# The last stage's begin set in another order: g products ahead of conversions, small weights in another PSUM bank, full products ahead of h products

## The chip, the core and the metric

The kernel runs on one core of one Trainium2 chip. Its engines are PE (matrix products), DVE, ACT and POOL (elementwise work) and SP, which issues the transfers. Each engine takes its instructions in the order of its own queue and waits at the first one whose inputs are not there. The metric is the time of one execution on the device in microseconds (us), the median of several runs.

## The reference

All of it is in float32; the weights of the last layer come as 64-bit floats and are converted on the chip.

```python
def reference(q, k, v, n_sink, window, phi, w1, w2, w_in, w_out):
    x = attention(q, k, v, n_sink, window)          # 4 x 768 tokens, 8 heads of 64
    x = x.reshape(3072, 512)
    logits = x @ phi                                # 3072 x 32
    d = softmax(logits, axis=0)
    s = (d.T @ x).reshape(8, 4, 512)
    o = relu(s @ w1) @ w2                           # 8 experts, 4 rows each
    x = softmax(logits, axis=1) @ o.reshape(32, 512)
    h = x @ w_in                                    # 3072 x 2048
    return (h - tanh(h)) @ w_out                    # 3072 x 512
```

## The kernel before

Attention, the routing and the experts take the first 227 us. The change concerns the last stage, the last two lines of the reference.

**The factors.** x has rank 32, so the kernel never forms it: the experts' output, transposed (`so`), is multiplied with w_in to a small matrix W of 32 x 2048, and h = c W with c the row softmax (`cT`). W is made by `w_mm(x)` in three parts, x = 0, 1, 2 with 128, 128 and 256 of 512 columns for each quarter of the partitions; they land in PSUM in `y`, in `cvt` and, the third, in the accumulator `o3` (`acc[3]`). `rows_a` (ACT) and `rows_b` (DVE) make from the first two the stationary tiles `wst0` and `wst1` of `hmm(0)` and `hmm(1)`; `whs_part` (ACT) and `wls_part` (DVE) split all three parts into a rounded and a rest part, from which `rows4` makes the other `wst`.

**A step.** Step s has a token chunk c of 512 tokens and a block f of 128 rows of w_out (f0 to f15). `hmm(s)` (PE, one matmul) makes h(s) in the PSUM bank `h0` or `h1`; `act_y(s)` makes on ACT a tanh and a square (`u`); `dve_part(s)` makes on DVE g(s), close to h - tanh(h) for the small h that occur; `split(s)` rounds it on ACT (`gh`) and takes the rest on POOL (`gl`). The product P(s) is `omm(s)`: for each of four accumulators `o0` to `o3` one matmul with gh and the block's `whi`, one with gh and `wlo`, one with gl and `whi`, 12 of 128x512. The first steps are (0,f0), (0,f1), (1,f0) to (1,f3), (0,f2) to (0,f5), (1,f4); at P1, P5 and P9 a group ends, the accumulators are evacuated (`evac`: o0 and o2 by ACT, o1 and o3 by DVE), and the next product overwrites them.

**A block.** Block f is converted from 64-bit words by `pre_conv(f, ops)`: four steps on DVE, "1", "2", "3", "g" (lines 116, 121, 126, 135), and a square on ACT, "s" (line 130). Then `wsplit(f)` takes POOL twice, for whi (line 1147) and wlo (line 1148). f0 and f1 are converted within SBUF, later ones by way of the PSUM bank `cvt`.

**The order.** Up to step 8 it is written out by hand: `step(s)` issues an older product `o`, then `hmm(s + 1)`, `act_y(s)`, `split(s - 1)`, then the evacuation of `o` if it ends a group, `dve_part(s)` with the conversions that `plan` has for s in between, and `wsplit`. `plan` is a table: step 3 has f2's second half, step 4 all of f3, steps 5 and 6 the halves of f4, step 7 all of f5, step 8 the first half of f6. From step 9 on a planner (`_Order`) sets the order of every engine by list scheduling: tasks carry a wished time, `LEAD`, `RCAST`, `TCAST`, `TLAG` and `TLAG2` say how far ahead of its use a thing is wished, and `BUSY` is the time for which it takes each engine to be still busy with the hand-written part. What it plans begins with P6. Behind step 31 the products go on with sums of blocks and of g's (a fast matrix product), to the end.

Of the kernel before, what the change touches and what calls it, by code (L numbers as in the profile page):

```python
# [10 lines left out]
F32 = mybir.dt.float32  # L11
# [5 lines left out]
AF = mybir.ActivationFunctionType  # L17
ALU = mybir.AluOpType
# [11 lines left out]
P = 128  # L30
# [26 lines left out]
CT = ((0, 4), (0, 6), (0, 7))  # L57
EPS_T = 0.0
US = {"tanh": 0.49, "mm": 0.2276, "h": 0.232, "act": 1.1, "cast": 0.49, "cast2": 0.3, "v": 0.6, "vs2": 0.34, "p": 1.26, "p2": 0.7, "pc": 0.7, "pch": 0.38, "ev": 0.49, "sq": 0.56}
LEAD, RCAST, SCAST, TCAST = 13.0, 6.0, 3.0, 6.0  # L60
RPS = 11
GGAP = 1.4
TLAG = 6.0
TLAG2 = 2.0
PAIRS = (((1, "P4"), (1, "P5")), ((1, "P7"), (1, "P1")), ((1, "P6"), (1, "P2")), ((1, "P3"), (2, "P4")),
         ((2, "P5"), (2, "P1")), ((2, "P7"), (2, "P6")), ((2, "P2"), (2, "P3")))
MULT = (("P4", "A22", "T4"), ("P5", "S1", "T1"), ("P7", "S3", "T3"), ("P1", "A11", "B11"), ("P6", "S2", "T2"), ("P2", "A12", "B21"), ("P3", "S4", "B22"))
# [77 lines left out]
class _Order:  # L145
# [1 line left out]
    LAT = {"PE": 0.2, "SP": 4.0, "ACT": 0.11, "DVE": 0.09, "POOL": 0.05}  # L147
    SELF = {"ACT": 0.12, "DVE": 0.12, "POOL": 0.12}
    PSUM = ("a0", "a1", "a2", "a3", "h0", "h1", "y", "cvt")
    BUSY = {"ACT": 0.3, "DVE": 2.7, "POOL": 3.8}  # L150

    def __init__(self):
        self.tasks = []
# [80 lines left out]
def tile_kernel(ctx: ExitStack, tc: tile.TileContext, qk, vv, v0, v0t, nw, phi, w1, w2,  # L234
                w_in, w_out, cst, gcst, out):
    nc = tc.nc
    PE, ACT, DVE, POOL, SP = nc.tensor, nc.scalar, nc.vector, nc.gpsimd, nc.sync
# [14 lines left out]
    def run(ctx, fast):  # L252
# [30 lines left out]
        for i in range(NR):  # L283
            pool, n = raw_p if i in RAW else ring2 if i in FREE else ring1, 1024 if i in HALF else 2048
# [739 lines left out]
        def raw_of(f):  # L1024
            return wraw[f % 6]
# [8 lines left out]
        acc = [pf.tile([P, 512], F32, name=f"o{t}") for t in range(4)]  # L1034
        y_t = pf.tile([P, 512], F32, name="y")
        cv_t = pf.tile([P, 512], F32, name="cvt")
# [3 lines left out]
        ca, cc = _cube(TAU * TAU)  # L1040
# [76 lines left out]
        whl = {}  # L1117
# [6 lines left out]
        wf, wf_b, cv_b, pcv = {}, [], [], {}  # L1124
# [8 lines left out]
        def pre_conv(f, ops):  # L1133
            if f not in pcv:
                wf[f] = wf_b[f if f < 8 else 8 + f % 3]
                pcv[f] = conv.start(raw_of(f), wf[f], cv_t if f > 1 else None)
            fns = {"1": conv.v1, "2": conv.v2, "3": conv.v3, "s": conv.sq, "g": conv.guard_dve,
                   "i": conv.ge_pool, "m": conv.mul_pool}
            for o in ops:
                fns[o](pcv[f])  # L1140

        def wsplit(f):
            hi, lo = whl[f]
            if f in WACT:
                ACT.copy(hi, wf[f])
            else:
                POOL.tensor_scalar(hi, wf[f], 1.0, 0.0, op0=ALU.mult, op1=ALU.add)  # L1147
            POOL.tensor_tensor(lo, wf[f], hi.bitcast(F32), op=ALU.subtract)
# [15 lines left out]
        for r in range(2):  # L1164
# [17 lines left out]
            for f in range(8):  # L1182
                for g in range(4):
                    i = 16 + 8 * r + 4 * (f // 4) + g
                    o, k = yo[NS * g:NS * g + NS, :], f
# [3 lines left out]
                    if k != f and f < 6:  # L1189
                        for x in range(2):  # L1190
                            PE.matmul(o[:, 256 * x:256 * x + 256], h, xt_t[2 * (k - 6) + x][:, 512:768],
                                      start=False, stop=False, skip_group_check=True)
# [17 lines left out]
            for x in range(2):  # L1210
# [3 lines left out]
                o = 16 * r  # L1214
# [7 lines left out]
        pre_conv(1, "s")  # L1222
        warm(WF[5])
        w_lo, w_n = (0, P, 2 * P), (P, P, 2 * P)
        W = [o[:, 0:n] for o, n in zip((y_t, cv_t, acc[3]), w_n)]
        w_st = [wa.tile([G3, n], F32R, name=f"wst{x}") for x, n in enumerate(w_n + (512, 512, 512))]

        def w_of(f):
            x, o = (f, 0) if f < 2 else (2, f - 2) if f < 4 else (2 + f // 4, f % 4)
            return w_st[x][:, P * o:P * o + P]  # L1230

        def w_mm(x):
            for f in range(4):
                for qd in range(4):
                    o = 512 * qd + w_lo[x]
                    PE.matmul(W[x][NS * qd:NS * qd + NS, :], so[f // 2][:, f % 2, :], win_t[:, f, o:o + w_n[x]],
                              start=f == 0, stop=f == 3)
# [14 lines left out]
        def h_of(s):  # L1252
            return h_b[s % 2]

        def hmm(s):
            c, f = steps[s][:2]
            PE.matmul(h_of(s), w_of(f), cT[0:G3, CK * c:CK * c + CK], start=True, stop=True)
# [1 line left out]
        w_mm(0)  # L1259
        rows_a(0)  # L1260
        rows_b(0)
        pre_conv(1, "12")
        w_mm(1)
        rows_a(1)
        hmm(0)
# [8 lines left out]
        def rows4(qd):  # L1274
            c = slice(0 if qd else 2 * P, 4 * P)
            for eng, g in ((POOL, 1), (DVE, 2), (ACT, 0)):
                dst = w_st[2 + qd][NS * g:NS * g + NS, :]
                src = (whs if g < 2 else wls)[NS * qd:NS * qd + NS, c]
                if eng is ACT:
                    ACT.copy(dst, src)  # L1280
                elif eng is DVE:
                    DVE.tensor_copy(dst, src)
                else:
                    POOL.tensor_scalar(dst, src.bitcast(F32), 1.0, 0.0, op0=ALU.mult, op1=ALU.add)

        def whs_part(x):
            ACT.copy(whs[:, w_lo[x]:w_lo[x] + w_n[x]], W[x])

        def wls_part(x):
            c = slice(w_lo[x], w_lo[x] + w_n[x])  # L1290
            DVE.tensor_tensor(wls[:, c], W[x], whs.bitcast(F32)[:, c], op=ALU.subtract)

# [8 lines left out]
        g_b, u_b = bufs("g", 3), bufs("u", 3)  # L1301
        gh_b, gl_b = bufs("gh", NG, F32R), bufs("gl", NG, F32R)
# [4 lines left out]
        def h_act(h, u, small):  # L1307
            if small:
                ACT.activation(h, h, AF.Tanh, scale=ca)
                ACT.activation(u, h, AF.Square, scale=cc ** 0.5)  # L1310
            else:
                ACT.activation(u, h, AF.Square)

        def act_y(s, small=True):
            h_act(h_of(s), u_b[s % 3], small)

        def split(s):
            g, gh, gl = g_b[s % 3], gh_b[s % NG], gl_b[s % NG]
            ACT.copy(gh, g)
            POOL.tensor_tensor(gl, g, gh.bitcast(F32), op=ALU.subtract)  # L1320

        def dve_part(s, small, fills):
            g_mul(h_of(s), u_b[s % 3], g_b[s % 3], small, fills)
# [26 lines left out]
        def omm(s, hi=True, lo=True, ts=range(4)):  # L1350
            c, f, first, last = steps[s]
            gh, gl = gh_b[s % NG], gl_b[s % NG]
            wh, wl = whl[f]

            def mm(t, a, w, start, stop):
                PE.matmul(acc[t], w[:, P * t:P * t + P], a, start=start, stop=stop)

            for t in ts:
                if hi:
                    mm(t, gh, wh, first, False)  # L1360
                    mm(t, gh, wl, False, False)
                if last and lo:
                    mm(t, gl, wh, False, True)
            if lo and not last:
                for t in ts:
                    mm(t, gl, wh, False, False)
# [40 lines left out]

        def step(s, small, pre):
            o = s - (DL + 1)
            if s < 5:  # L1410
                o = 1 if s == 3 else -1
            if o == 1:
                omm(1, lo=False, ts=(0, 1))
                for t in range(4):
                    omm(1, hi=False, ts=(t,))
                    if t < 2:
                        omm(1, lo=False, ts=(t + 2,))
            elif o >= 0:
                omm(o)
            hmm(s + 1)  # L1420
            todo = plan.get(s, ())
            fills = []
            act_y(s, small)
            split(s - 1)
            if o >= 0 and steps[o][3]:
                fills += evac(o)
            for f, ph in todo:
                fills += [lambda f=f, p=p: pre_conv(f, p) for p in ("3g" if ph else "12")]
                if not ph:
                    pre_conv(f, "s")  # L1430
            dve_part(s, small, fills)
            for f, ph in todo:
                if ph:
                    wsplit(f)
                    if f + 6 < 16:
                        wload(f + 6)
            if s in row_at:
                rows4(row_at[s])
# [3 lines left out]
        while turns:  # L1442
            n = 2 if s_ % 3 == 1 and turns[0][0] < 8 else 1
# [1 line left out]
            s_ += 1  # L1445

        act_y(0)
        w_mm(2)
        early.close()
        fq = ctx.enter_context(tc.tile_pool(name="fq", bufs=1))  # L1450
        w_split_tiles(fq, range(NB, 16))
        dve_part(0, True, ())
        pre_conv(1, "3")
        wload(7)
        split(0)
        pre_conv(1, "g")
        wsplit(1)
        hmm(1)
        omm(0, lo=False, ts=(0, 1, 2))
        whs_part(2)  # L1460
        wls_part(2)
        act_y(1)
        omm(0, lo=False, ts=(3,))
        dve_part(1, True, ())
        for x in range(2):
            whs_part(x)
            wls_part(x)
        hmm(2)
        omm(0, hi=False)
        split(1)  # L1470
        act_y(2)
        rows4(0)
        pre_conv(2, "1s")
        dve_part(2, True, (lambda: pre_conv(2, "2"),))
        hmm(3)
        for s in range(3, S0):
            step(s, True, True)
# [320 lines left out]
        for k, u in enumerate(units):  # L1798
            if u[0] != "r" and prods[u[1]][2] in ("T1", "T2"):
                j, o, i = nt % 3, 0 if u[1] == "P5" else 256, u[2]  # L1800
# [8 lines left out]
        for s, todo in plan.items():  # L1809
            if s < S0:  # L1810
                continue
            t = op(s - DL - 1)
            for e, (f, ph) in enumerate(todo):
# [12 lines left out]
                else:  # L1826
                    add(tb, "DVE", US["v"], rw + ["cvt"], ["cvt"], lambda cv=cv: conv.v3(cv))
                    add(tb + 0.5, "DVE", US["v"], [q, "cvt"], wn, lambda cv=cv: conv.guard_dve(cv))
                    hi, lo = whl[f]
# [4 lines left out]
                    if f >= 8:  # L1834
# [8 lines left out]

                        tb += TLAG if f < 13 else TLAG + TLAG2 * (f - 12)
                        tsub(tb, B1[:, lo_], [l_], B1[:, hi_], B1[:, lo_], [r_, l_])
# [6 lines left out]
        for s, qd in row_at.items():  # L1852
            if s >= S0:
                t = op(s - DL - 1)
# [7 lines left out]
        if fast:  # L1862
            t = op(18)
            add(t, "ACT", US["cast"], ["whs"], ["z"], lambda: ACT.activation(z, whs, AF.Square))
            add(t + 1, "DVE", US["v"], ["z"], ["wmax"], lambda: DVE.tensor_reduce(wmax, z, axis=AX.X, op=ALU.max))
            t = op(N + 100)
# [109 lines left out]
```

## Time and profile before

| | us |
|---|---|
| median of 3 runs | 507.75 |
| the runs | 507.40, 507.75, 510.46 |
| the profiled execution | 508.94 |
| span of its instructions | 507.0 |
| PE busy in the span | 480.7 (95%) |
| DVE, ACT, POOL busy | 414.6, 385.9, 301.6 |

The span is the time from the first to the last instruction of the profiled execution; the execution itself is 1.9 us longer. A matmul's busy time overlaps the next one's, so starts and not lengths tell how fast PE goes. A share of busy time is a mean over stages with different limits.

### The profile page before, as it was taken

To read this page: it belongs to the slowest core of one execution; us is meant where nothing else is said; L and a number is where in the kernel's file an instruction comes from. 1 tells how busy PE (TensorE), PEld (TensorE's weight loads), DVE (VectorE), ACT (ScalarE), POOL (GpSimd) and SP (SyncE) were. 2 spreads that over 40 slices of the span, in tenths; PEclk is the share of its full clock that TensorE was granted. 3 is DMA by queue.
4 is the path that set the end of the run, shared out by engine and by line. 5 is a ranking of instruction groups with operands and counts; after the bars stand their busy time and mean duration, and the time that the engine had idled before them with its cause. 6 is when DMAs were issued, how large, how long until landed. Compare 5 with 4: busy or idle time off the path is not lost.

```text
span 507.0 us, 10286 instructions
## 1 busy us (share of the span) xinstructions
PE 480.7 (95%) x3558; PEld 336.7 (66%) x3558; DVE 414.6 (82%) x826; ACT 385.9 (76%) x1084; POOL 301.6 (59%) x366
## 2 busy tenths in 40 slices
PE   8799999899998999798999999999999999999995
PEld 4565655555555633235688888888888888888884
DVE  2999998998998559659999999788858798965892
ACT  4889998998999414337898987998768998855750
POOL 0466755765654100005899998358747794789871
PEclk9999999999999999899999999999999999999998
DMA  8989976532385999994433000220000030100022
GB/s 298 414 332 349 348 300 244 178 132 95 106 296 185 307 313 404 410 406 154 124 100 109 1 0 2 83 84 1 1 0 0 2 125 1 41 2 0 1 85 87
DMA packets 22139, 77.60 MB, mean 153 GB/s; under 512 B 2882, under 2 KB 4034, under 8 KB 20162
## 3 DMA queue, kind: packets, MB, share of 16 engines
q1 hardware_dynamic: 22082, 76.89, 41.4%
q8 instruction: 29, 0.48, 0.4%
q14 instruction: 28, 0.23, 0.1%
HBM read 70.59 MB, written 6.29 MB: 152 GB/s over the span
## 4 chain that ended last, share of the span: by engine, by line
PE 66%; DVE 10%; ACT 10%; DMA 8%; POOL 3%; issue 2%; DVEq 0%; POOLq 0%; SPq 0%; ACTq 0%
PE o L1507 44%; DMA w<-in_w 4%; ACT w L702 4%; PE sc L672 3%; PE o L1088 3%; PE av L767 2%; DMA w<-in_qk 2%; PE h L1576 2%; ACT w L686 2%; DVE mx L693 2%; DMA w<-in_w_out 2%; PE pT L735 2%; DVE w L749 1%; PE mi L530 1%; POOL gl L1320 1%
## 5 line engine op out<-in xcount | busy, mean ns | idle before, releaser
L1507 PE MATMUL o<-gh,whi 128*128 128x512 f32 x232 | 91.2, 393 | 0.0
L1507 PE MATMUL o<-gh,wlo 128*128 128x512 f32 x232 | 90.9, 392 | 0.0
L712 POOL TENSOR_TENSOR w<-w,su 128x528 f32<-128x528 f32 x38 | 40.6, 1068 | 52.4 <-DVE su L709 37.5
L1507 PE MATMUL o<-gl,whi 128*128 128x512 f32 x232 | 71.6, 390 | 0.0
L1499 POOL TENSOR_TENSOR gl<-w,gh 128x512 fp32r<-128x512 f32 x39 | 51.3, 1322 | 26.5 <-ACT gh L1645 15.5
L702 ACT ACTIVATE w<-w,nb 128x132 f32<-128x132 f32 x152 | 59.6, 393 | 1.2
L1507 PEld LDWEIGHTS o<-gh,whi 128*128 128x128 f32 x232 | 43.7, 188 | 9.9 <-ACT mk L1705 0.2
L1507 PEld LDWEIGHTS o<-gh,wlo 128*128 128x128 f32 x232 | 43.6, 188 | 9.7
L1507 PEld LDWEIGHTS o<-gl,whi 128*128 128x128 f32 x232 | 43.6, 188 | 9.5
L767 PE MATMUL av<-w,w 128*64 128x256 f32 (+1 forms) x448 | 48.3, 344 | 0.0
L672 PE MATMUL sc<-w 64*64 64x200 f32 (+2 forms) x768 | 44.8, 331 | 2.3 <-DMA w<-in_qk 1.4
L1147 POOL TENSOR_SCALAR whi<-wx 128x512 fp32r<-128x512 f32 x6 | 3.7, 619 | 62.8 <-DMA w<-in_w_out 61.0
L767 PEld LDWEIGHTS av<-w,w 128*64 128x64 f32 x448 | 25.8, 136 | 16.4 <-issue 10.7
L672 PEld LDWEIGHTS sc<-w 64*64 64x64 f32 x768 | 26.1, 132 | 15.1 <-issue 9.9
L1334 DVE TENSOR_TENSOR h<-u,h 128x512 f32<-128x512 f32 x40 | 27.6, 691 | 10.0 <-ACT u L1588 9.9
L1645 ACT CAST gh<-h 128x512 fp32r<-128x512 f32 x40 | 23.6, 590 | 11.1 <-DVE w L1499 4.2
L749 DVE TENSOR_TENSOR w<-pT,c_t 128x512 f32<-128x512 f32 x46 | 31.3, 680 | 0.0
L1645 ACT CAST gh<-w 128x512 fp32r<-128x512 f32 x39 | 24.2, 621 | 7.9 <-PE o L1507 7.6
L686 ACT COPY w<-sc 128x264 f32<-128x264 f32 x63 | 21.1, 373 | 11.9 <-PE sc L803 6.1
L1499 DVE TENSOR_TENSOR gl<-h,gh 128x512 fp32r<-128x512 f32 x40 | 27.4, 685 | 2.7 <-ACT gh L1645 2.0
L702 ACT ACTIVATION_READ_ACCUMULATOR w<-w,nb 128x1 f32 x152 | 28.3, 186 | 0.0
L693 DVE TENSOR_REDUCE mx<-w 128x4 f32<-128x528 f32 x38 | 26.7, 703 | 1.3
(388 smaller groups left out, 1332.2 us busy)
## 6 DMA issues: line engine op xcount, KB each, us to landing
w<-in_w SPq DMA_DIRECT2D x30, 512.0 KB, 10.2
w<-in_w SPq DMA_DIRECT2D x14, 1024.0 KB, 6.5
w<-in_qk SPq DMA_DIRECT2D x16, 780.0 KB, 6.1
w<-in_w_out SPq DMA_DIRECT2D x16, 512.0 KB, 3.6
w<-in_vv SPq DMA_DIRECT2D x16, 384.0 KB, 4.0
w<-in_w_in SPq DMA_DIRECT2D x8, 512.0 KB, 4.8
out<-xt SPq DMA_DIRECT2D x12, 256.0 KB, 2.0
win_t<-in_w_in SPq DMA_DIRECT2D x4, 512.0 KB, 9.5
```

Source lines behind the costliest of these rows:

```text
L672: PE.matmul(sc_t[i][u][w, o:o + n], a[r, 64 * j:64 * j + 64], kslc(a, lo, n)[r, :], start=True, stop=True)
L686: ACT.copy(z, base)
L693: DVE.tensor_reduce(mx, Z, axis=AX.X, op=ALU.max)
L702: ACT.activation(Z[:, u, :], Z[:, u, :], AF.Exp, bias=nb[:, u:u + 1], scale=SCALE, accum_out=su[:, u, :])
L712: (POOL if i < NQ - 1 else DVE).tensor_tensor(Z, Z, su.to_broadcast([P, 4, CH]), op=ALU.mult)
L749: DVE.tensor_tensor(d[:, :, 0, :], src, mL, op=ALU.mult)
L767: PE.matmul(dst[r, :], v[:, t, r], l, start=start, stop=stop, skip_group_check=True)
L1088: PE.matmul(ha[x][NS * g:NS * g + NS, :], sT[f // 2][:, f % 2, :], ring_t(i + g, o, 512), start=f == 0, stop=f == 3)
L1334: DVE.tensor_tensor(g, u, h, op=ALU.mult)
L1499: td.any_of(at, {e: (us[e], lambda e=e: names[e].tensor_tensor(dst, a, b, op=alu), len(engs) > 1 or sbuf) for e in engs}, rd, wr)
L1507: PE.matmul(o, w, a, start=start, stop=stop)
L1645: add(at, "ACT", US["cast"], [gn], [f"gh{x}"], lambda: ACT.copy(gh_b[x], g))
```

## The change

`w_mm` takes a list of the parts f of its inner sum, and its third part now lands in the free columns of the bank `y` instead of in `o3`. h(1) is issued between the two halves of the third part, and its tanh and square are issued around the cast of g(0). g(0) and g(1) stand on DVE ahead of f1's conversion steps "2" and "3", "g". P0 is issued whole, its gh part and h(2) and its gl part. f1's whi is made by ACT, its wlo and gl(1) by DVE, and no longer by POOL. P1 takes all whi matmuls first. From step 4 on every hand-written product is issued one step sooner: `o = s - 2`, in steps 3 to 7, and step 8 issues none, so that P2 stands ahead of h(5), P3 ahead of h(6), to P5 ahead of h(8). `plan` is the same. f2's step "2" moves from the DVE part of step 2 to step 3, behind the evacuations. The planner's LEAD, TCAST, TLAG2 and BUSY have other values, by which it sets another order behind P6.

```diff
-LEAD, RCAST, SCAST, TCAST = 13.0, 6.0, 3.0, 6.0
+LEAD, RCAST, SCAST, TCAST = 10.0, 6.0, 3.0, 7.0
-TLAG2 = 2.0
+TLAG2 = 0.0
-    BUSY = {"ACT": 0.3, "DVE": 2.7, "POOL": 3.8}
+    BUSY = {"ACT": 0.8, "DVE": 3.7, "POOL": 4.2}
...
-        W = [o[:, 0:n] for o, n in zip((y_t, cv_t, acc[3]), w_n)]
+        W = [y_t[:, 0:P], cv_t[:, 0:P], y_t[:, P:3 * P]]
...
-        pre_conv(1, "12")
+        pre_conv(1, "1")
...
+        def h_tanh(s):
+            ACT.activation(h_of(s), h_of(s), AF.Tanh, scale=ca)
+
+        def h_sq(s):
+            ACT.activation(u_b[s % 3], h_of(s), AF.Square, scale=cc ** 0.5)
...
         def step(s, small, pre):
             o = s - (DL + 1)
-            if s < 5:
-                o = 1 if s == 3 else -1
+            if s < 9:
+                o = s - 2 if s < 8 else -1
             if o == 1:
-                omm(1, lo=False, ts=(0, 1))
+                (gh, wh), (gl, wl) = ((x[1], y) for x, y in zip((gh_b, gl_b), whl[1]))
                 for t in range(4):
-                    omm(1, hi=False, ts=(t,))
-                    if t < 2:
-                        omm(1, lo=False, ts=(t + 2,))
+                    PE.matmul(acc[t], wh[:, P * t:P * t + P], gh, start=False, stop=False)
+                for t in range(5):
+                    if t < 4:
+                        PE.matmul(acc[t], wl[:, P * t:P * t + P], gh, start=False, stop=False)
+                    if t:
+                        PE.matmul(acc[t - 1], wh[:, P * (t - 1):P * t], gl, start=False, stop=True)
...
+            if s == 3:
+                fills[2:2] = [lambda: pre_conv(2, "2")]
             dve_part(s, small, fills)
...
         act_y(0)
-        w_mm(2)
+        w_mm(2, (0, 1))
+        hmm(1)
+        w_mm(2, (2, 3))
...
         dve_part(0, True, ())
+        h_tanh(1)
+        pre_conv(1, "2")
+        split(0)
+        h_sq(1)
+        dve_part(1, True, ())
         pre_conv(1, "3")
         wload(7)
-        split(0)
-        pre_conv(1, "g")
-        wsplit(1)
-        hmm(1)
-        omm(0, lo=False, ts=(0, 1, 2))
-        whs_part(2)
-        wls_part(2)
-        act_y(1)
-        omm(0, lo=False, ts=(3,))
-        dve_part(1, True, ())
         for x in range(2):
             whs_part(x)
-            wls_part(x)
+        pre_conv(1, "g")
+        omm(0, lo=False)
         hmm(2)
         omm(0, hi=False)
-        split(1)
+        ACT.copy(gh_b[1], g_b[1])
+        whs_part(2)
+        ACT.copy(whl[1][0], wf[1])
+        for x in (0, 1, 2):
+            wls_part(x)
+        DVE.tensor_tensor(whl[1][1], wf[1], whl[1][0].bitcast(F32), op=ALU.subtract)
+        DVE.tensor_tensor(gl_b[1], g_b[1], gh_b[1].bitcast(F32), op=ALU.subtract)
         act_y(2)
         rows4(0)
+        dve_part(2, True, ())
         pre_conv(2, "1s")
-        dve_part(2, True, (lambda: pre_conv(2, "2"),))
         hmm(3)
```

What stands on DVE ahead of the first product, before (L116 to L135 are the conversion steps of f1 in `wx0`, g0 is made from u0 and the bank h0):

```order
L116 TENSOR_SCALAR wx0_133<-w2_0_116 128x512
L121 SCALAR_TENSOR_TENSOR wx0_133<-w2_0_116,wx0_133 128x512
L1246 TENSOR_TENSOR wst1_3220<-cvt_2878,wst1_3220 32x128
L1334 TENSOR_TENSOR g0_3282<-u0_3285,h0_2871 128x512
L126 SCALAR_TENSOR_TENSOR wx0_133<-w2_0_116,wx0_133 128x512
L135 SCALAR_TENSOR_TENSOR wx0_133<-cv_3142,wx0_133 128x512
```

And the same place of DVE now:

```order
L116 TENSOR_SCALAR wx0_133<-w2_0_116 128x512
L1246 TENSOR_TENSOR wst1_3220<-cvt_2878,wst1_3220 32x128
L1340 TENSOR_TENSOR g0_3281<-u0_3284,h0_2871 128x512
L121 SCALAR_TENSOR_TENSOR wx0_133<-w2_0_116,wx0_133 128x512
L1340 TENSOR_TENSOR g1_3282<-u1_3285,h1_2872 128x512
L126 SCALAR_TENSOR_TENSOR wx0_133<-w2_0_116,wx0_133 128x512
L135 SCALAR_TENSOR_TENSOR wx0_133<-cv_3142,wx0_133 128x512
```

The last part of `wst1`, which h(1) needs, and g(0) moved ahead of f1's second step, and g(1) ahead of its third.

DVE around the evacuation of P5, before (the two copies of o1 and o3 are the evacuations; `w4` is the raw f5 and `w2` the raw f6 here, `wx1` takes the converted block):

```order
L121 SCALAR_TENSOR_TENSOR cvt_2878<-w4_0_118,cvt_2878 128x512
L126 SCALAR_TENSOR_TENSOR cvt_2878<-w4_0_118,cvt_2878 128x512
L135 SCALAR_TENSOR_TENSOR wx1_134<-cv_3142,cvt_2878 128x512
L1378 COPY h1_2882<-o1_2874 128x512
L1334 TENSOR_TENSOR g2_3284<-u2_3287,h0_2871 128x512
L1378 COPY c_t_68<-o3_2876 128x512
L116 TENSOR_SCALAR cvt_2878<-w2_0_116 128x512
```

And the same evacuation on DVE now:

```order
L1384 COPY h1_2882<-o1_2874 128x512
L1340 TENSOR_TENSOR g1_3282<-u1_3285,h1_2872 128x512
L1384 COPY c_t_68<-o3_2876 128x512
L116 TENSOR_SCALAR cvt_2878<-w4_0_118 128x512
L121 SCALAR_TENSOR_TENSOR cvt_2878<-w4_0_118,cvt_2878 128x512
L126 SCALAR_TENSOR_TENSOR cvt_2878<-w4_0_118,cvt_2878 128x512
L135 SCALAR_TENSOR_TENSOR wx1_134<-cv_3142,cvt_2878 128x512
L116 TENSOR_SCALAR cvt_2878<-w2_0_116 128x512
```

All four conversion steps of f5 stood ahead of the two evacuations of P5 and now stand behind them; POOL's row for this place is the same as before: whi5, wlo5, then gl(7).

## Rows read from the trace of the kernel before

**Rows 1.** Busy time by stretch (first of all engines, then of PE alone), granted clock, DMA.

```profile
255.40:320.00 64.60, 64.60 (x282) 52.68 (x282) 61.71 (x102) 56.79 (x111) 61.62 (x74) 1.00 0.15 50
...
255.40:501.00 245.60, 245.60 (x1070) 1.00 0.10 34
...
204.00:210.00 6.00, 4.07 (x22) 0.76 1.03 410
```

**Rows 2.** The chain that ended last, 247 to 262 us: start, length, what.

```profile
248.95 1.45 POOL gl L1320
...
251.19 1.30 POOL gl L1320
...
255.61 2.76 PE o L1507 x12
...
261.37 0.23 PE h L1576
```

**Rows 3.** Timeline of PE, 222 to 274 us: start, length, instruction, [idle before].

```profile
230.20 1.93 PE L1236 MATMUL o<-win_t,so 128*32 128x256 f32 x32
...
233.94 0.47 PE L1356 MATMUL o<-gh,whi 128*128 128x512 f32 x1 [0.85 <-ACT gh L1319]
234.25 0.40 PE L1356 MATMUL o<-gh,wlo 128*128 128x512 f32 x1
...
252.54 0.50 PE L1356 MATMUL o<-gl,whi 128*128 128x512 f32 x1 [0.18 <-POOL gl L1320]
...
255.45 0.40 PE L1507 MATMUL o<-gh,whi 128*128 128x512 f32 x1
...
268.57 0.39 PE L1507 MATMUL o<-gh,whi 128*128 128x512 f32 x1
```

**Rows 4.** Timeline of ACT, 222 to 274 us.

```profile
230.99 0.60 ACT L1310 ACTIVATE u<-h 128x512 f32<-128x512 f32 x1
...
233.22 0.62 ACT L1319 CAST gh<-g 128x512 fp32r<-128x512 f32 x1 [1.64 <-DVE g L1334]
...
239.08 0.60 ACT L1310 ACTIVATE u<-h 128x512 f32<-128x512 f32 x1
239.87 0.62 ACT L1319 CAST gh<-g 128x512 fp32r<-128x512 f32 x1 [0.19 <-DVE g L1334]
240.40 1.10 ACT L1380 COPY xt<-o 128x512 f32<-128x512 f32 x2
...
267.80 0.60 ACT L1705 COPY mk<-o 128x512 f32<-128x512 f32 x1
```

**Rows 5.** Timeline of DVE, 222 to 274 us.

```profile
230.50 1.65 DVE L121 SCALAR_TENSOR_TENSOR wx<-w,wx 128x512 uint32<-128x512 uint32 x1
...
232.50 0.69 DVE L1334 TENSOR_TENSOR g<-u,h 128x512 f32<-128x512 f32 x1
...
242.74 0.69 DVE L135 SCALAR_TENSOR_TENSOR wx<-lg,cvt 128x512 f32<-128x512 f32 x1
...
254.05 0.69 DVE L135 SCALAR_TENSOR_TENSOR wx<-cv,cvt 128x512 f32<-128x512 f32 x1
254.65 0.68 DVE L1378 COPY h<-o 128x512 f32<-128x512 f32 x1
...
256.45 0.68 DVE L116 TENSOR_SCALAR cvt<-w 128x512 uint32<-128x512 uint32 x1
257.17 0.69 DVE L121 SCALAR_TENSOR_TENSOR cvt<-w,cvt 128x512 uint32<-128x512 uint32 x1
...
270.18 0.68 DVE L1499 TENSOR_TENSOR gl<-h,gh 128x512 fp32r<-128x512 f32 x1
```

**Rows 6.** Timeline of POOL, 222 to 262 us.

```profile
230.28 1.33 POOL L1148 TENSOR_TENSOR wlo<-wx,whi 128x512 fp32r<-128x512 f32 x1
...
243.52 0.62 POOL L1147 TENSOR_SCALAR whi<-wx 128x512 fp32r<-128x512 f32 x1 [1.60 <-DVE wx L135]
...
245.48 1.31 POOL L1320 TENSOR_TENSOR gl<-g,gh 128x512 fp32r<-128x512 f32 x1
```

More of the change, by code (lines that the diff above doesn't have):

```diff
@@ L1230, in w_of, with w_mm @@
             return w_st[x][:, P * o:P * o + P]
-        def w_mm(x):
-            for f in range(4):
+        def w_mm(x, fs=range(4)):
+            for f in fs:
                 for qd in range(4):
```

## The prediction

> **Names.** P(k) is the product of step k (12 matmuls), h(k) the matmul that feeds it, g(k) its value, gh(k) and gl(k) the two halves, f0, f1, ... the blocks of w_out; whi, wlo are a block's halves. Times are microseconds from the start of the span.
>
> **What bounds the kernel now.** First I read the busy time by stretch. From 255.4 to 501 PE is busy 245.60 of 245.60 us with 1070 matmuls [rows 1], one every 0.23 us: no wait is left there, so nothing in that stretch can become faster by order alone. Everything that this change can win lies between the small weights (about 228) and the first product of the planner (P6, 255.45 [rows 3]). Then the chain of waits: just ahead of P6 it runs through POOL (gl4 until 250.40, gl5 until 252.49 [rows 2]), and P5 resumes at 252.54 after an idle stop on POOL's gl [rows 3]. So the begin is bound by POOL's queue, and this queue by the DVE conversions that feed it. Between the first product's start, 233.94, and P6 lie 81 matmuls, 18.7 us at 0.231; the stretch takes 21.51 us, so PE waits 2.8 us in it. That, and an earlier first product, is the whole prize: under 4 us of 507, below the 1% (about 5 us) that a measurement of this kernel can tell from no change.
>
> **First product.** Before, DVE's second step on f1 stands ahead of g(0); it stretched to 1.65 us (230.50 to 232.15) because POOL's wlo ran until 231.61 [rows 5, 6]. So g(0) started at 232.50 although its square ended at 231.59 [rows 4, 5]. After, g(0) stands ahead of that step: start 231.63, ACT's cast 0.72 later (233.22 - 232.50) at 232.35, first product another 0.72 later (233.94 - 233.22 [rows 3, 4]) at 233.07: **-0.87**. The third small-weight product splits: 32 matmuls took 1.93 [rows 3], half of it then h(1) at about 231.1, the other half by 232.4, ahead of 233.07: nothing. A copy of f1's halves moves from POOL to ACT and DVE, gl(1) from POOL to DVE: no cost by itself, but these now stand in DVE's queue ahead of f2.
>
> **The walk of DVE up to f2.** Independent DVE operations start 0.60 apart (254.05 to 254.65), dependent conversion steps 0.72 (256.45 to 257.17 [rows 5]). h(1) at 231.1 gives its square by 233.47, g(1) 233.51. f1's third step at 234.12 meets POOL's gl(0) (233.05 to 234.35) and, as the 1.65 us step did, ends 0.54 after it, 234.89; the fourth ends 235.61. Three small wls 0.75; whi1 on ACT until 236.26 (0.62, the length of a cast [rows 4]); wlo1 236.30, gl(1) 236.90, small copy 237.50, g(2) 237.95, f2's first step 238.55, evacuation 239.15, g(3) 239.75, evacuation 240.35, then f2's second to fourth step 240.95, 241.67, 242.39 to 243.08. Before, the fourth step of f2 started at 242.74 [rows 5]. In spite of all that moved, POOL gets f2 **only 0.35 earlier**: whi2 at 243.17 instead of 243.52 [rows 6]. From whi2 on POOL has the same row of work (whi2, wlo2, gl3, whi3, wlo3, gl4, wst, gl5), which took 3.27 to gl3's end (245.48 + 1.31 [rows 6]), 6.88 to gl4's and 8.97 to gl5's end [rows 2]: after, gl3 is there at 246.44, gl4 250.05, gl5 252.14.
>
> **The walk of PE.** A restart costs 0.10 more (233.94 to 234.25 instead of 0.21 to 0.23 [rows 3]). Starting at 233.07, P1 is due at 236.38 and whi1 is just there. P2 is due at 239.39, but it overwrites what ACT must evacuate: before, the square of h(3) started at 239.08, the cast at 239.87, the two evacuations at 240.40 [rows 4]; after, this row starts about 0.33 earlier and without the idle time ahead of the cast, first evacuation done 240.37, P2 240.47: wait 1.08. P3's gl part is due at 245.42, gl3 lands 246.49: wait 1.07. P4's due 249.60, gl4 250.10: wait 0.50. P5's due 251.82, gl5 252.19: wait 0.37. With 0.10 for each restart, P6 starts at 255.06. Before it was 255.45, with one more h issued (0.23): equal work is done 0.16 earlier. **Most of the early start is gone again.**
>
> **The new wait.** P5 moved one step up, f5's conversions did not. Before, DVE's fourth step of f5 was at 254.05, ahead of P5's evacuation at 254.65 [rows 5]. After, both evacuations of P5 stand ahead of all four steps of f5 in DVE's queue (second pair of listings), and the second evacuation needs P5's end. P5's last matmul starts 254.36, its sum is there 254.76; evacuation 254.79, f5's steps 255.39, 256.11, 256.83, 257.55 to 258.24; POOL's whi5 258.33, gl7 1.96 later (245.48 - 243.52) at 260.29 and done 261.60, since POOL has wlo5 ahead of it. PE meanwhile issues h(8), h(9), P6 and y, starts P7 at 258.06 and is at gl7 at 259.91: wait 1.74, restart 0.10. The calculation counts from P5's end alone, so it holds wherever P5 ends. **This is the largest single term.**
>
> **Behind it.** DVE is done with the old order's last step (257.17 before [rows 5]) at 259.5, ACT's casts follow it, and PE is later by less. At P10 before, ACT's second evacuation ended at 268.40 and the matmul that waits for it started at 268.57 [rows 3, 4]: 0.17 to spare. I take 0.35 of new waits there, between 0 and 1.5. A gain is excluded, since PE has no wait there to lose [rows 1]. The other lags (LEAD, TCAST, TLAG2, BUSY) reorder POOL, ACT and DVE behind P6; the last 30 rows of PE are the same.
>
> **Sum.** -0.87 (first product) - 2.80 (old waits) + 0.08 + 1.08 + 1.07 + 0.50 + 0.37 + 1.74 + 0.50 (five restarts) + 0.35 = **+2.0 us**. Bounds: the start between -0.9 and 0; the waits for gl3 to gl5 together between 0.5 (if f2's steps come 0.5 earlier) and 3.0; gl7 between 1.4 (steps 0.60 apart) and 2.2 (POOL's gl at 1.45 [rows 2]). The profiled execution took 508.94 with a span of 507.0, above the median of the runs, 507.75; the sum is a difference of spans, so I put it on the median: **509.8**, own range 508.6 to 511.0.
>
> [...]
>
> **Rivals.**
> *The new order works.* If DVE reaches f2 a microsecond earlier than I walk it (its 0.60 steps hide more than I see), gl3 and gl5 stop nobody, and if DVE can take f5 before P5's evacuations bind, P7 doesn't wait: 2.0 - 1.07 - 1.74 - 0.20 = -1.0, 506.7 (505.0 to 508.2). The floor, with no wait left at all, is -3.7: 504.1. For it: the first product surely comes earlier. Against it: DVE's order around P5, which a queue in order cannot escape.
> *It doesn't do what it says:* g(0) waits for something else and the first product stays at 233.94; then PE waits 0.87 less later, since POOL's row decides: again 509.8. It has no chance of its own.
> *Slower, by the lag.* LEAD falls from 13 to 10: counted in the order, h(12) now stands 40 matmuls (9.2 us) ahead of P12, before 52 (12.0). Before, from h(12) at 261.37 [rows 2] to gl(12) at 270.86 [rows 5] it took 9.5 us, on a DVE that is busy 61.71 of 64.60 [rows 1]. P12 needs gl(12) 1.85 after its start, so it decides once that way takes over 11.05: DVE is 2.3 late there. At 14 us it would add 3: 512.8, and more where DVE cannot catch up (to 516).
> [...]
>
> **How the numbers follow.** Forecast 0.55; the order works 0.28; the lag 0.11, half of it beyond 1%; the clock 0.06. The range 506.2 to 511.6 leaves out the lower part of the second (0.1) and most of the lag. Faster by over 1% (under 502.7) lies below the floor: 0.01; slower by over 1% (above 512.8): 0.06; within: 0.93.
>
> **What would show it.** Right: first product near 233.1; P2 stopped by an evacuation on ACT; POOL's whi2 near 243.2; whi5 more than 3 us after P5's end; PE idle 1 to 2 us on POOL's gl in P7, near 260; no idle PE after about 272. Wrong: whi2 before 242.2, or f5's fourth step before P5's second evacuation; or PE idle after 280, which the lag would bring.

## The result: 0.6% slower

The changed kernel takes 511.19 us (median of 4, 510.54 to 511.76), the kernel before 507.57 in the same runs: a ratio of **1.0063, 95% interval 1.0038 to 1.0087**, that is +3.2 us (1.9 to 4.4); the two medians alone differ by 3.6. Forecast were +2.0 and 509.8; 511.19 lies inside the range of 506.2 to 511.6 and just above the forecast's own 508.6 to 511.0. The direction, the place and five of six stops came as worked out, one term was a microsecond too small. The profiled execution took 510.80 with a span of 508.9.

The two profiles begin the last stage at different times, before anything that the change touches. The first small-weight product of the kernel before:

```profile
227.87 1.08 PE L1236 MATMUL y<-win_t,so 128*32 128x128 f32 x32 [0.15 <-DVE so L1216]
```

PE of the changed kernel from there, every row that the timeline marks with idle time before it (and P6's first, 253.92), to be held against [rows 3]:

```profile
226.73 1.08 PE L1236 MATMUL y<-win_t,so 128*32 128x128 f32 x32 [0.16 <-DVE so L1216]
...
231.91 0.47 PE L1362 MATMUL o<-gh,whi 128*128 128x512 f32 x1 [0.36 <-issue]
...
239.23 0.50 PE L1362 MATMUL o<-gh,whi 128*128 128x512 f32 x1 [0.81 <-ACT xt L1386]
...
245.30 1.20 PE L1362 MATMUL o<-gl,whi 128*128 128x512 f32 x4 [0.95 <-POOL gl L1326]
...
248.95 1.21 PE L1362 MATMUL o<-gl,whi 128*128 128x512 f32 x4 [0.36 <-POOL gl L1326]
...
251.01 0.50 PE L1362 MATMUL o<-gl,whi 128*128 128x512 f32 x1 [0.15 <-POOL gl L1326]
...
253.92 0.39 PE L1522 MATMUL o<-gh,whi 128*128 128x512 f32 x1
...
260.52 1.20 PE L1522 MATMUL o<-gl,whi 128*128 128x512 f32 x4 [1.63 <-POOL gl L1326]
...
269.01 0.47 PE L1522 MATMUL o<-gh,whi 128*128 128x512 f32 x1 [1.07 <-DVE xt L1713]
```

Counted from that first row, the first product starts at 5.18 (before 6.07), P6 at 27.19 (before 27.58, where one h more, 0.23, was issued ahead of it), and the span ends at 282.2 (before 279.1). So 0.16 is won up to P6 and 3.2 lost behind it, at two stops alone: P7 (start to start 2.02 instead of 0.23) and P10 (1.47). From P6 to the end PE is busy all but 2.7 us, where it was busy throughout before [rows 1]:

```profile
253.92:501.00 247.08, 244.38 (x1062) 1.00 0.09 33
```

Behind the first of the two stops stand DVE and POOL; the rows for [rows 5, 6] of the changed kernel, DVE first:

```profile
252.24 0.69 DVE L1384 COPY h<-o 128x512 f32<-128x512 f32 x1 [2.46 <-PE o L1362]
...
253.60 0.69 DVE L1384 COPY c_t<-o 128x512 f32<-128x512 f32 x1
...
256.46 0.69 DVE L135 SCALAR_TENSOR_TENSOR wx<-cv,cvt 128x512 f32<-128x512 f32 x1
...
257.78 0.68 DVE L1340 TENSOR_TENSOR g<-u,h 128x512 f32<-128x512 f32 x1
...
262.51 0.69 DVE L1340 TENSOR_TENSOR g<-u,y 128x512 f32<-128x512 f32 x1 [1.52 <-ACT u L1603]
...
268.18 0.68 DVE L1713 TENSOR_TENSOR xt<-o,xt 128x512 f32<-128x512 f32 x1
```

```profile
242.01 0.62 POOL L1147 TENSOR_SCALAR whi<-wx 128x512 fp32r<-128x512 f32 x1 [1.88 <-DVE wx L135]
...
257.23 0.62 POOL L1147 TENSOR_SCALAR whi<-wx 128x512 fp32r<-128x512 f32 x1 [3.06 <-DVE wx L135]
...
259.18 1.28 POOL L1326 TENSOR_TENSOR gl<-g,gh 128x512 fp32r<-128x512 f32 x1
```

DVE idles 2.46 for P5's sum in `o1`, evacuates twice, and only then converts f5 (fourth step 256.46; before it stood at 254.05, ahead of the evacuation). POOL idles 3.06 for that step, and gl(7), which needs nothing of f5, stands behind both halves of f5. The same burst holds back g(8) (257.78). On ACT, P2's evacuation and the cast that waits for g(8), for [rows 4]:

```profile
238.59 1.08 ACT L1386 COPY xt<-o 128x512 f32<-128x512 f32 x2
...
258.50 0.62 ACT L1660 CAST gh<-g 128x512 fp32r<-128x512 f32 x1 [1.74 <-DVE g L1340]
```

How this reaches P10 is told by the chain of the changed kernel (for [rows 2]; start, length, what), from f5's fourth step on:

```profile
256.46 0.70 DVE wx L135
...
257.78 0.69 DVE g L1340
258.50 0.62 ACT gh L1660
259.11 0.49 ACT u L1603
259.61 0.56 ACT cv L130
260.19 0.62 ACT wst L1876
260.81 0.48 ACT y L1602
261.31 0.62 ACT wst L1876
261.93 0.50 ACT u L1603
```

Behind the cast of gh(8) the planner has ACT do a conversion's square and two small-weight copies ahead of, or between, the tanh and the square of h(10), which lies in bank `y`. DVE idles 1.52 for that square (262.51), runs back to back from there, and reaches the evacuation of P9 at 268.18. P10 overwrites what is evacuated. In the kernel before, this evacuation on DVE ended 1.56 us ahead of P10's first matmul:

```profile
265.40 0.68 DVE L1698 TENSOR_TENSOR xt<-o,xt 128x512 f32<-128x512 f32 x1
...
267.64 0.39 PE L1507 MATMUL o<-gh,whi 128*128 128x512 f32 x1
```

### The profile page after: what moved, and what is told of

Read it like the earlier page. It is cut to its first block, busy times and chain, and to the rows that moved or that the text cites. A ratio compares the mean times of both kernels' runs of the same rounds, so it can differ in the third digit from the quotient of the medians.

```text
span 508.9 us, 10255 instructions
## 1 busy us (share of the span) xinstructions
PE 478.4 (94%) x3558; PEld 336.8 (66%) x3558; DVE 410.6 (81%) x826; ACT 386.4 (76%) x1090; POOL 296.5 (58%) x360
## 4 chain that ended last, share of the span: by engine, by line
PE 63%; DVE 15%; ACT 11%; DMA 6%; issue 2%; POOL 2%; SPq 1%; DVEq 0%; POOLq 0%; ACTq 0%
PE o L1522 42%; ACT w L702 4%; PE o L1088 3%; PE av L767 3%; PE sc L672 3%; DMA w<-in_qk 2%; PE h L1591 2%; DVE mx L693 2%; ACT w L686 2%; DMA w<-in_w_out 2%; PE pT L735 2%; DMA w<-in_vv 2%; DVE w L749 1%; PE mi L530 1%; PE y L1591 1%
## 5 line engine op out<-in xcount | busy, mean ns | idle before, releaser
L1602 ACT ACTIVATE h<-h 128x512 f32<-128x512 f32 x46 | 27.0, 592 | 6.5 <-PE h L1591 6.1
L1340 DVE TENSOR_TENSOR h<-u,h 128x512 f32<-128x512 f32 x37 | 25.5, 690 | 5.6 <-ACT u L1603 5.5
L1603 ACT ACTIVATE u<-h 128x512 f32<-128x512 f32 x46 | 27.6, 607 | 0.7
L1514 DVE TENSOR_TENSOR gl<-h,gh 128x512 fp32r<-128x512 f32 x37 | 25.3, 684 | 3.4 <-ACT gh L1660 3.4
```

The costliest lines, as they stand in the source:

```text
L1340: DVE.tensor_tensor(g, u, h, op=ALU.mult)
L1514: td.any_of(at, {e: (us[e], lambda e=e: names[e].tensor_tensor(dst, a, b, op=alu), len(engs) > 1 or sbuf) for e in engs}, rd, wr)
L1602: add(at, "ACT", US["tanh"], [b[1]], [b[1]], lambda: ACT.activation(b[0], b[0], AF.Tanh, scale=ca))
L1603: add(at + 0.1, "ACT", US["cast"], [b[1]], [un], lambda: ACT.activation(u, b[0], AF.Square, scale=cc ** 0.5))
```

## The experiments

The ratio is to the kernel before, measured beside it; in brackets the 95% interval.

| run | ratio | us against before |
|---|---|---|
| changed kernel | 1.0063 [1.0038, 1.0087] | +3.2 |
| e1_gl7_first | 1.0072 [1.0055, 1.0089] | +3.7 |
| e2_f5_first | 1.0040 [1.0026, 1.0055] | +2.0 |
| e3_old_lags | 1.0079 [1.0065, 1.0092] | +4.0 |
| e4_busy_seen | 1.0038 [1.0024, 1.0052] | +1.9 |
| e5_before_new_lags | 1.0007 [0.9998, 1.0016] | +0.4 |
| e6_before_g0 | 0.9995 [0.9987, 1.0004] | -0.3 |
| e7_f5_busy | 1.0002 [0.9993, 1.0011] | +0.1 |
| e8_pool | 1.0033 [1.0020, 1.0046] | +1.7 |
| e9_g7 | 1.0017 [1.0007, 1.0028] | +0.9 |
| e10_fit | 1.0000 [0.9991, 1.0010] | 0.0 |
| e11_g8 | 0.9971 [0.9962, 0.9981] | -1.5 |

### P7's stop alone: e1 and e2

e1 (changed kernel, f5's halves behind gl(7) on POOL):

```diff
             split(s - 1)
+            if s == 8:
+                wsplit(5)
...
-                if ph:
+                if ph and s != 7:
                     wsplit(f)
```

> The changed kernel, with gl(7) ahead of f5's two halves in POOL's queue; nothing else moves on DVE, ACT or PE. Both theories say that P7's stop on POOL's gl (1.63 us idle at 260.52) is gone, since gh(7) is cast by 255.70 and POOL is free then. Theory 'one chain': the stop at P10 is DVE's queue (its row of work runs back to back from 262.51 to the evacuation at 268.18), and that queue doesn't hear of POOL's order; PE only gets there earlier and waits there for longer, 2.3 to 2.9 us idle instead of 1.07, and the time is 2.4 to 3.2 above the kernel before (the changed kernel: 3.2 above). Rival 'terms that add', as in the sum of the prediction: P10's stop stays at 1.07, and the time is 1.4 above the kernel before.

P7 no longer stops, and nothing is won (+3.7, interval 2.8 to 4.5). PE's only stops behind P6:

```profile
265.12 0.50 PE L1525 MATMUL o<-gl,whi 128*128 128x512 f32 x1 [0.69 <-POOL gl L1517]
269.58 0.47 PE L1525 MATMUL o<-gh,whi 128*128 128x512 f32 x1 [1.67 <-DVE xt L1716]
```

P10's idle time grew from 1.07 to 1.67, and a new stop of 0.69 came in P9; together 2.36, as 'one chain' expected for P10 alone, and the time lies above its 2.4 to 3.2. DVE's evacuation starts 41.49 after the first small weight (41.45 in the changed kernel). So my sum's way, in which terms add, was wrong here: P7's stop hid behind P10's, whose time DVE sets.

e2 (changed kernel, DVE does three of f5's steps in the 2.46 us that it idled):

```diff
+            if s == 7:
+                pre_conv(5, "123")
+                fills[2:] = [lambda: pre_conv(5, "g")]
             dve_part(s, small, fills)
```

> The changed kernel, with the first three of f5's four DVE steps ahead of P5's two evacuations, in the 2.46 us that DVE idled ahead of 252.24; the fourth step stays behind them. Theory 'one chain' (f5's steps behind the evacuations made DVE late, and through g(8), gh(8) and y's tanh on ACT also the evacuation of P9): DVE's fourth step starts near 254.3 instead of 256.46, gl(7) is there before P7 needs it, DVE is some 2 us earlier at P10: both stops gone (idle below 0.3 each), 3.0 less, so 0.0 to 0.5 above the kernel before. Rival 'the lags': P10's stop is the planner's order and stays or grows as PE gets there earlier; 1.4 to 3.2 above the kernel before.

Here 1.2 of the 3.2 is gone (2.0 left): P7's stop went at its root, so DVE came forward together with PE. But P10's stop stayed (267.64, idle 1.18), against "one chain": all but one of f5's steps are gone from behind the evacuations, and the stop is not.

### The planner: e3, e4, e5, e7

e3 is the changed kernel with the four numbers of the planner as before; e4 has only other BUSY times:

```diff
-LEAD, RCAST, SCAST, TCAST = 10.0, 6.0, 3.0, 7.0
+LEAD, RCAST, SCAST, TCAST = 13.0, 6.0, 3.0, 6.0
-TLAG2 = 0.0
+TLAG2 = 2.0
-    BUSY = {"ACT": 0.8, "DVE": 3.7, "POOL": 4.2}
+    BUSY = {"ACT": 0.3, "DVE": 2.7, "POOL": 3.8}
```

```diff
-    BUSY = {"ACT": 0.8, "DVE": 3.7, "POOL": 4.2}
+    BUSY = {"ACT": 2.3, "DVE": 5.1, "POOL": 6.5}
```

> The changed kernel with the scheduler's numbers of before (LEAD 13, TCAST 6, TLAG2 2, BUSY 0.3, 2.7, 3.8); the begin up to P5 is the changed one. Theory 'one chain': P7's stop stays (1.6 idle), P10's stays between 0.5 and 1.5, since DVE is late from its own queue; 2.6 to 3.7 above the kernel before. Rival 'the lags': P10's stop is gone with the new numbers, 2.0 above the kernel before or less.

> The changed kernel, with the times at which the planner takes ACT, DVE and POOL to be free after P6's start set to what its trace shows (2.3, 5.1 and 6.5 us instead of 0.8, 3.7 and 4.2). P7's stop is written by hand and stays. Theory 'the planner is told a wrong time': knowing how late the engines are it puts the work that P10 needs first, P10's idle falls below 0.5, the time is 2.0 to 2.7 above the kernel before. Rival 'late is late': there is no work to put behind, P10's idle stays near 1.1, 3.2 above the kernel before.

The old lags help nothing (+4.0, above the 2.6 to 3.7 of 'one chain'). P10's idle stayed at 1.02 as expected; P7's stop did not: a stop of 1.49 ahead of a planned h at 258.60 took its place, since with LEAD 13 that h stands earlier in PE's queue, and its row names a late g on DVE as what it waited for. e4 takes 1.3 off (+1.9, just under the 2.0 forecast): P7's stop stays (1.61) and P10's is gone, with no stop behind it. Its ACT and DVE rows:

```profile
259.02 0.59 ACT L1602 ACTIVATE y<-y 128x512 f32<-128x512 f32 x1
259.54 0.65 ACT L130 ACTIVATE cv<-w 128x512 f32<-128x512 f32 x1
260.10 0.58 ACT L1603 ACTIVATE u<-y 128x512 f32<-128x512 f32 x1
260.70 1.25 ACT L1876 CAST wst<-whs 32x512 fp32r<-32x512 f32 x2
```

```profile
260.78 0.69 DVE L1340 TENSOR_TENSOR g<-u,y 128x512 f32<-128x512 f32 x1 [0.27 <-ACT u L1603]
...
265.45 0.69 DVE L1713 TENSOR_TENSOR xt<-o,xt 128x512 f32<-128x512 f32 x1
```

The copies now stand behind the square of h(10); g(10) and the evacuation come 1.25 and 2.25 sooner, counted from the first small weight (which is 0.48 earlier here). Engines as late as in the changed kernel, but in another order: P10's stop is the planner's, which was told too early times. That ACT's 0.8 is the one that matters is likely from these rows, but not shown: all three were changed together.

e5 is the kernel before with the new numbers (e3's diff the other way round, nothing else):

> The kernel before, with the scheduler's new numbers alone (LEAD 10, TCAST 7, TLAG2 0, BUSY 0.8, 3.7, 4.2); its begin is the old one. Theory 'the numbers only have to fit the begin': PE has at most one short stop behind P6, 0.0 to 0.7 above the kernel before. Rival 'the lags cost': h comes too late behind P6 with LEAD 10, PE idles in several places behind P10, 1 or more above.

PE doesn't stop behind P6, and the interval, -0.1 to 0.8 us, leaves the lags under a microsecond. e7 is e2 with other times:

```diff
-    BUSY = {"ACT": 0.8, "DVE": 3.7, "POOL": 4.2}
+    BUSY = {"ACT": 2.3, "DVE": 2.9, "POOL": 4.3}
```

> The changed kernel with three of f5's steps ahead of P5's evacuations (as in the run with that edit alone, 2.0 above the kernel before, idle at P10 1.18), and the planner's times set to what that run's trace shows behind P6's start (ACT 2.3, DVE 2.9, POOL 4.3; the changed kernel has 0.8, 3.7, 4.2, so ACT's is the one that was wrong). Theory 'P10's stop comes from the planner's times': idle at P10 below 0.3, no stop behind P6, 0.2 to 0.9 above the kernel before. Rival 'P10's stop is DVE's own row of work': it stays, 2.0 above.

No stop behind P6 that the timeline marks, and +0.1: **the two stops are the whole loss**. Which of the three times matters wasn't taken apart; from e2 to e7 ACT's moved by 1.5, DVE's down by 0.8, POOL's by 0.1.

### The early start: e6

The kernel before with g(0) ahead of f1's second step:

```diff
-        pre_conv(1, "12")
+        pre_conv(1, "1")
...
-        pre_conv(1, "3")
+        pre_conv(1, "23")
```

> The kernel before, with g(0) ahead of DVE's second step on f1, and nothing else of the change: the first product starts as early as in the changed kernel. Theory 'POOL and DVE set the begin': the first product comes 0.9 earlier, PE waits as much longer ahead of P5, and P6 starts within 0.4 of where it did; 0.4 below to 0.2 above the kernel before. Rival 'an early start is kept': 0.9 below.

```profile
231.93 0.47 PE L1356 MATMUL o<-gh,whi 128*128 128x512 f32 x1 [0.48 <-issue]
234.59 0.50 PE L1356 MATMUL o<-gh,whi 128*128 128x512 f32 x1 [1.06 <-DVE wls L1291]
```

The first product comes at 5.19 from the first small weight instead of 6.07; then PE waits 1.06 in P0 for DVE's `wls`, which reads the third small weight out of `o3`. (The changed kernel has it in the bank `y`.) Of 0.88, 0.25 is left at P6 (27.33 from the first small weight, before 27.58); the time, -0.3 with an interval of -0.7 to 0.2, can't tell this from nothing.

### A version that beats both: e8 to e11

e8 takes on the stops ahead of P6 in e2: on POOL the gl's ahead of the halves of blocks, with f2 to f5 split one step later, and the copy of `rows4(1)` behind gl(5); on ACT o0's evacuation ahead of h(3)'s tanh and the casts of gh(5) to gh(7) ahead of the next tanh; P3 to P5 take their whi first; BUSY is 2.3, 5.1, 5.5.

```diff
+        halves = {4: 2, 5: 3, 7: 4, 8: 5}
...
+            if s == 3:
+                evac(1, (0,))
+                split(2)
+                fills += evac(1, (2,))
+                act_y(3)
+            elif s < 6:
+                h_tanh(s)
+                split(s - 1)
+                h_sq(s)
+            else:
+                split(s - 1)
+                act_y(s, small)
...
+            if s in halves:
+                wsplit(halves[s])
```

> As the run above it, and the stops ahead of P6 taken on: in POOL's queue gl(3), gl(4), gl(6), gl(7) stand ahead of the halves of f2, f3, f4, f5; ACT evacuates o0 ahead of h(3)'s tanh, and casts gh(5) to gh(7) ahead of the next step's tanh; P3 and P4 do their whi matmuls ahead of wlo, P5 goes like P1; the third small copy moves behind gl(5); planner's times 2.3, 5.1, 5.5. Theory 'order of POOL's and ACT's queues': the stops of P2, P3 and P4 go (2.8 with their restarts), P5 keeps up to 0.8, P6 starts some 2.5 sooner after the first product; 2.8 to 1.2 below the kernel before. Rival 'DVE is the bound': DVE, 2.5 further behind at P6's start, stops PE after it instead, and the time is 0 to 0.9 above the kernel before.

The stops of P2 to P4 went and P5 kept 0.23, as expected; but h(9) waited 2.37 for g(7), which now stood behind three of f5's steps, and PE came out of that stop slow, one matmul in 0.43. At +1.7 neither the theory's range nor the rival's holds. Its timeline around it, and its windows (busy time, matmuls, granted clock):

```profile
255.03 0.56 PE L1257 MATMUL h<-cT,wst 96*128 96x512 f32 x1 [2.37 <-DVE g L1340]
...
255.82 0.63 PE L1550 MATMUL o<-gh,wlo 128*128 128x512 f32 x1
256.25 0.63 PE L1550 MATMUL o<-gh,whi 128*128 128x512 f32 x1
...
258.79 1.09 PE L1550 MATMUL o<-gl,whi 128*128 128x512 f32 x4
```

```profile
250.00:255.00 5.00, 2.44 (x10) 1.00 0.36 108
255.00:259.00 4.00, 3.97 (x10) 0.57 0.41 131
259.00:262.00 3.00, 3.00 (x14) 1.00 0.56 169
```

e9 is e8 with f5 behind the evacuations again and tanh, cast, square in steps 4 to 7; e10 is e9 with BUSY alone set anew:

```diff
-            if s == 7:
-                pre_conv(5, "123")
-                fills[2:] = [lambda: pre_conv(5, "g")]
...
-            elif s < 6:
+            elif s < 8:
                 h_tanh(s)
...
-    BUSY = {"ACT": 2.3, "DVE": 5.1, "POOL": 5.5}
+    BUSY = {"ACT": 3.2, "DVE": 5.5, "POOL": 5.2}
```

```diff
-    BUSY = {"ACT": 3.2, "DVE": 5.5, "POOL": 5.2}
+    BUSY = {"ACT": 3.0, "DVE": 5.5, "POOL": 5.8}
```

> As the run with gl ahead of the blocks' halves (1.9 above the kernel before; PE's stops ahead of P5's end gone, but 2.37 idle ahead of h(9), on DVE's g(7), which stood behind three of f5's steps, and its clock at 0.58 and 0.56 for 4 us behind that stop), with g(7) sooner: f5's steps all behind P5's evacuations again (POOL's gl(7) no longer stands behind f5's halves), and on ACT the cast of the step before between tanh and square in steps 4 to 7; planner's times 3.2, 5.5, 5.2. Theory 'the queue that g(7) stands in': h(9) waits under 0.6, the clock stays at 1.00, and what the begin won is kept: 2.8 to 1.2 below the kernel before. Rival 'DVE is the bound': DVE is 2 to 3 us later against PE at P6 than in the kernel before, and PE stops behind P6 for it; 0.5 below to 0.9 above the kernel before.

> As the run with g(7) sooner (0.9 above the kernel before; there P9 waited 0.79 for gl on POOL, P10 0.84 for ACT's copy, and the clock ran at half speed for about 4 us behind these two stops), with the planner's times alone set anew, at or a little above what that run's trace shows (ACT 2.6, DVE 5.1, POOL 5.3): 3.0, 5.5, 5.8. Theory 'P9's and P10's stops are the planner's order, as P10's was in the changed kernel': both under 0.3, the clock stays at 1.00 behind 255, and the time is 3.6 below that of the run with g(7) sooner, 2.0 to 2.9 below the kernel before. Rival 'DVE is the bound': the stops stay or come back further behind, 0.0 to 0.9 above the kernel before.

e9 starts P6 at 25.26 from the first small weight (changed kernel 27.19), h(9) waits 0.44; then P9 and P10 stop for 0.79 and 0.84, with the clock at 0.57 for 4 us behind them (last section). Its time, +0.9, misses the theory's range and lies at the end of the rival's. The profiled execution took 510.25, the median is 508.36: whether the clock fell in the others too is not known. e10 loses the stop at P10 and the slow clock, not the one in P9 (0.69), and is level: short of its forecast by two. Its ACT row gave a reason, 1.50 of idle time for g(8), which is late from f5's steps and which the planner takes as done:

```profile
256.87 0.62 ACT L1685 CAST gh<-g 128x512 fp32r<-128x512 f32 x1 [1.50 <-DVE g L1340]
```

e11 is e10 with g(7) ahead of P5's evacuations and g(8) ahead of f5's fourth step, the squares of steps 6 and 7 ahead of the casts, and BUSY 3.2, 6.1, 6.5:

```diff
+            if s in (7, 8):
+                dve_part(s, small, ())
+            if s == 8:
+                pre_conv(5, "g")
```

> As the run with the planner's times set anew (level with the kernel before; PE idle 0.46 ahead of h(9), 0.69 in P9 on gl, 0.18 near 287, 0.95 and 0.85 from start to start in the first two), with g(7) ahead of P5's evacuations and g(8) ahead of the fourth of f5's steps in DVE's queue, ACT's squares of steps 6 and 7 ahead of the casts of the step before, and the planner's times moved to 3.2, 6.1, 6.5, since P6 should start 0.6 sooner. In the run before it ACT waited 1.50 for g(8), which the planner holds for done. Theory 'ACT behind g(8)': h(9) doesn't wait, ACT's idle time ahead of gh(8) falls below 0.6, P9's stop below 0.3, no stop over 0.5 behind it; 0.6 to 2.0 below the kernel before. Rival 'DVE is the bound': as much is lost again behind P6, 0.5 below to 0.9 above.

```profile
255.70 0.62 ACT L1698 CAST gh<-g 128x512 fp32r<-128x512 f32 x1
```

ACT no longer idles ahead of gh(8), P6 starts at 24.63, and the timeline of PE from the first product to 340 marks one stop, 0.23 in P5. **0.9971 [0.9962, 0.9981], 1.5 us faster than the kernel before.** "DVE is the bound" has fallen in the main: P6 starts 2.6 sooner than in the changed kernel (27.19) with the same work on DVE ahead of it, and with the right order PE still makes no marked stop behind it. Not all of it is kept: against the kernel before, P6 is 2.7 sooner at equal work (27.58 less the one h, 0.23), and 0.8 is lost again behind it, at two waits too short to be marked and their restarts: P10's start on ACT's evacuation (264.49, start to start 0.42) and a matmul that waits for a late value of DVE (286.61, 0.51). What each of e11's three edits is worth wasn't taken apart.

## Why the prediction was right, and where it was short

- **First product:** -0.89, forecast -0.87.
- **The walk of DVE to f2:** whi2 at 15.28 from the first small weight, forecast 15.30. f1's third step took 0.79 and ended 0.55 after POOL's gl(0) (233.74 against 233.19), forecast 0.54; in e8 it took 0.79 and ended 0.54 after it (235.18 against 234.64).
- **P2 to P5:** start to start beyond the usual 0.23 by 0.98, 1.11, 0.52, 0.32; forecast 1.08, 1.07, 0.50, 0.37. P6 at 27.19, forecast 27.19; to the hundredth that is luck, since errors of up to 0.10 cancel. "Most of the early start is gone again" holds, by e6 too, though there another wait took it.
- **The new wait:** 1.79, forecast 1.74, with whi5 more than 3 us after P5's end. The mechanism was right (e2: DVE's order), but not that its price stands by itself: e1 took it away and won nothing.
- **Behind it** is the mis-sized term: 0.35 forecast (0 to 1.5), 1.24 and a restart of 0.08 measured. The 0.35 was a guess: I had the lateness of DVE and let it eat the 0.17 of slack that ACT's second evacuation had at P10. The stop came at DVE's first, which had 1.56 to spare. I did not hold my own walk against BUSY: by it gl(7) ends 6.5 after P6's start and f5's burst holds ACT's casts, while the planner sets its order for 4.2 and 0.8. e4 and e7 show that this order, not the lateness, was the stop. With 1.32 in its place the sum is +3.0, which agrees with the timing (+3.2).
- **Slower, by the lag:** fallen (e3, e5). **The new order works:** not as written; without its two stops it is level (e7), and only with e8's to e11's further edits is it faster.
- **Slower, by the clock** (chance 0.06, that PE's clock falls behind P7's stop): not here; the granted clock was 1.00 behind P7's stop of 1.63 (260.6 to 263). In e8 it fell: behind 2.37 the clock was 0.57 (255 to 259), and nine matmuls in a row took 3.76 us from start to start (255.03 to 258.79) instead of 2.07 (nine times 0.23), 1.7 lost. In e9 it was 0.57 too, behind shorter stops (last section).

## What to carry to other kernels

Where a hand-written part runs into a planned one, walk every engine's hand-written queue to its end and hold it against the times that the planner assumes: here that mismatch cost 1.3 of 3.2 us (e4). In an in-order queue, put what the next product needs ahead of what a later one needs (gl ahead of the next block's halves, g ahead of conversions: so in e8 and e11, among other edits), and take away stops at their root, since one removed on another engine's queue may only move, as in e1. Compare profiles from the last row that a change can't touch, not from the start of the span: here these rows lay up to 2 us apart between runs.

## What the runs showed that I had not expected

PE's clock fell to 0.57 not only behind one stop of 2.37 us (e8) but also behind two of 0.79 and 0.84, 2 us apart (e9), while one of 1.63 (changed kernel) left it at 1.00.

PE of e9, then its windows:

```profile
264.90 1.20 PE L1547 MATMUL o<-gl,whi 128*128 128x512 f32 x4 [0.79 <-POOL gl L1539]
...
266.93 0.67 PE L1547 MATMUL o<-gh,whi 128*128 128x512 f32 x1 [0.84 <-ACT q L1745]
```

```profile
262.00:267.00 5.00, 3.37 (x14) 1.00 0.35 103
267.00:271.00 4.00, 4.00 (x11) 0.57 0.16 23
```

Nine matmuls took 3.75 us from start to start behind the second stop (266.93 to 270.68) instead of 2.07, so it cost 1.7 more than its own length.

A stop's length alone doesn't settle it. From 204 to 210 us, ahead of all that the change touches, both kernels have the same instructions; the granted clock was 0.76 there before [rows 1], with a wait of 1.93 on PE, and 1.00 in the changed kernel, with one of 2.99. The row in the kernel before, the row in the changed one, and the changed one's window (all engines):

```profile
206.40 1.26 PE L1159 MATMUL o<-c_t,ck 128*96 128x128 f32 x8 [1.93 <-DVE ck L1155]
```

```profile
206.51 1.08 PE L1159 MATMUL o<-c_t,ck 128*96 128x128 f32 x8 [2.99 <-DVE ck L1155]
```

```profile
204.00:210.00 6.00, 2.93 (x24) 1.25 (x24) 5.44 (x13) 1.66 (x3) 0.00 (x0) 1.00 1.02 408
```

The 24 matmuls behind that wait, 8 of L1159 and then 16 of L1194, took 2.93 us in the changed kernel and in e3 (wait of 2.92), but 4.57 in the kernel before, 4.58 in e1 (2.62), 4.49 in e2 (2.50) and 4.25 in e4 (2.97). So a profile shows what the clock did in that execution; what decides it stays open.
